# A list schedule for a gated two-layer block: other issue order, folded w_phi, accumulated kv, token-major queries

## The chip, the cores and the metric

The kernel runs on one NeuronCore of a Trainium2 chip, and the metric is the device time of one execution in microseconds (us). The core has a matrix engine (PE, with its weight loads shown as PEld), a vector engine (DVE), an activation engine (ACT), a general engine (POOL) and a queue for transfers (SP). Each takes its own instructions strictly in the order in which the program issues them, and waits for the others by semaphores. Matmul results land in PSUM, which this kernel hands out in eight tiles of up to 512 fp32 columns.

## The reference

There are S = 2048 tokens of D = 512 features. A vector c gives six modulation rows; sa, ca, ga steer the attention half and sb, cb, gb the feed-forward half.

```python
h = _layernorm(x, axis=-1) * (1 + ca) + sa
x = x + ga * _A_ref(h, A_wqkv, A_w_phi, A_wo)
h = _layernorm(x, axis=-1) * (1 + cb) + sb
x = x + gb * _B_ref(h, B_w_gate, B_w_up, B_w_down)
```

`_A_ref` is a linear attention with 32 heads of 16 features. Queries and keys are multiplied by a 16x16 matrix w_phi of their head; phi is the softmax of the result beside the softmax of its negative. For each head kv = sum over tokens of phi_k times v, z = sum of phi_k; the output is (phi_q kv) / (phi_q z + 1e-6), times wo. `_B_ref` is silu(h w_gate) * (h w_up), times w_down, with 1376 hidden features. All keys must be seen before the first query can be finished, and a token's feed-forward half needs its attention output.

## The kernel before

Tokens are handled in 16 tiles of 128 rows, or in 4 chunks of 512. The stages stand in the program in this order, and each engine gets its instructions in that order.

1. **Setup.** The modulation columns come from one-column matmuls (L138). w_phi is folded into wq and wk: 32 transposes (L176), 32 matmuls against a block-diagonal w_phi (L183), with (1 + ca) multiplied into the result (L186) and into wv (L188). The terms with sa become biases: cq for the queries (L192), a row ck added to the keys by a matmul with a row of ones (L200, L266), bv added to kv afterwards (L206, L370). Layernorm statistics of all 16 tiles (L216 to L223) are issued before the first key tile.
2. **Keys.** For each pair of tiles `k_ln_pair` normalises, transposes and copies (L256 to L259); for each tile `k_tile_mm` makes keys and values (L265, L269), two exponentials (L271, L272), the values' copy (L275), head sums (L278), reciprocals (L280) and phik on POOL (L282). phik and vaug are kept for all 16 tiles. Four of the 16 `q_front_j` groups (L291, L295) are placed among the key tiles.
3. **Between.** `prep_mod2`, `prep_bgu`, the multiplication of wg and wu by (1 + cb) on ACT (L347, L348), of wo and wd by their gates on DVE (L351, L356), and `kv_group`: eight runs of 16 matmuls over the token tiles (L365).
4. **Query side of a chunk**, `q_back_gen`: it works feature-major. Sums of the exponentials come from eight matmuls with a selection matrix (L391) and four fp32 transposes (L398); the quotients are made on DVE (L401 to L415), transposed back (L419), spread over the features by eight matmuls with Esel (L428), multiplied into the exponentials (L431) and taken through KVblk (L436); then wo (L446), the residual (L448), the second layernorm (L233) and its transposes (L236, L237).
5. **Feed-forward of a chunk**: 11 groups of `ffn_gu` (L469 gate, L473 up, L476 silu, L479 on DVE or L483 and L484 on ACT and POOL), then 4 `ffn_down` (L492) and the output (L496, or L499 and L500).

The order of 4 among 3 and 5 is written by hand: `plan` mixes the 12 other query groups with the first chunk's `q_back_gen`, and `hooks_m` and `hooks_t` say after which group the next chunk's generator takes a step. The first `ffn_gu` waits for the first chunk's last step.

## Time and profile before

| what | value |
|---|---|
| three timed runs | 277.44, 277.82 and 278.03 us, median 277.82 |
| span of the profiled execution | 275.5 us |
| the profiled execution's own time | not given; the median lies 2.3 us above the span |
| PE busy | 240.7 us, 87% of the span, 1468 matmuls |
| DVE, ACT, POOL busy | 171.8, 138.6, 80.5 us |
| read from memory | 11.58 MB |

The span runs from the first to the last instruction of the profiled execution. Busy is time in which at least one instruction of an engine runs; matmuls overlap, so that the mean time of one (384 ns) is longer than the step from one to the next (four in 0.86 us). An engine's idle time matters only where the end depends on it.

### The profile page before, as it was taken

What the parts mean: (1) busy time and instruction counts of PE and PEld (TensorE: products, weight loads), DVE (VectorE), ACT (ScalarE), POOL (GpSimd) and SP (SyncE); (2) the same over time, 40 slices, a digit from 0 to 9 for tenths busy, and PEclk for the clock granted to TensorE, in tenths of its full rate; (3) what the DMA queues carried; (4) which work ended last, traced back from release to release, by engine and by line L of the source; (5) the groups of instructions that cost most, each with busy time, mean ns of one, the idle gap of its engine ahead of it and who ended that gap; (6) DMA issues with size and microseconds to landing.
All of it is one profiled execution on the core that took longest, in us unless ns stands there. A gap on an engine that the chain in (4) does not pass through costs nothing.

```text
span 275.5 us, 3831 instructions
## 1 busy us (share of the span) xinstructions
PE 240.7 (87%) x1468; PEld 118.5 (43%) x1468; DVE 171.8 (62%) x351; ACT 138.6 (50%) x208; POOL 80.5 (29%) x91
## 2 busy tenths in 40 slices
PE   0499869999799879289999899999899999899993
PEld 0473323433586334234444344444344444444441
DVE  4799899999859946716665627556718555712210
ACT  2297146775696956056691056651055660165500
POOL 2602267576870000102221312230313310233311
PEclk9999999999979979869999999999999999999999
DMA  7999600000000000000000010000000000100001
GB/s 260 385 403 411 228 0 2 0 2 2 0 2 4 0 0 2 0 0 0 0 2 19 19 38 2 0 1 20 33 27 0 0 2 19 38 21 0 0 19 57
DMA packets 10067, 13.91 MB, mean 51 GB/s; under 512 B 993, under 2 KB 6978, under 8 KB 10050
## 3 DMA queue, kind: packets, MB, share of 16 engines
q1 hardware_dynamic: 9522, 13.16, 12.9%
q10 hardware_dynamic: 528, 0.52, 0.6%
q8 instruction: 11, 0.18, 0.3%
q14 instruction: 6, 0.05, 0.1%
HBM read 11.58 MB, written 2.10 MB: 50 GB/s over the span
## 4 chain that ended last, share of the span: by engine, by line
PE 47%; issue 17%; DVE 14%; POOL 8%; ACT 8%; DMA 3%; POOLq 1%; SPq 0%
PE g_ps L469 14%; PE u_ps L473 13%; PE f_ps L492 9%; POOL phik L282 5%; DVE Ssum L278 4%; DMA wqkv_sb<-in_A_wqkv_dram 3%; ACT xn2T L237 3%; POOL ln_rstd L221 3%; DVE Rk L280 2%; PE a_ps L446 2%; PE sdT_ps L391 2%; PE cb_ps L428 2%; PE o_ps L436 2%; DVE ln_st L216 1%; DVE vaug L275 1%
## 5 line engine op out<-in xcount | busy, mean ns | idle before, releaser
L469 PE MATMUL g_ps<-xn2T,wg_sb 128*128 128x512 bf16 (+1 forms) x176 | 46.0, 384 | 2.1 <-ACT xn2T L237 2.0
L473 PE MATMUL u_ps<-xn2T,wu_sb 128*128 128x512 bf16 (+1 forms) x176 | 45.9, 384 | 0.0
L479 DVE SCALAR_TENSOR_TENSOR gu<-u_ps,bgu,sg 128x512 bf16<-128x512 f32 (+1 forms) x24 | 18.0, 750 | 41.7 <-PE u_ps L473 39.5
L484 POOL TENSOR_TENSOR gu<-u_sb,sg 128x512 bf16<-128x512 bf16 x20 | 23.5, 1176 | 69.3 <-ACT u_sb L483 69.3
L476 ACT ACTIVATE sg<-g_ps,bgu 128x512 bf16<-128x512 f32 (+1 forms) x44 | 30.3, 688 | 26.4 <-PE g_ps L469 25.4
L492 PE MATMUL f_ps<-wd_sb,gu 128*128 128x512 bf16 (+1 forms) x176 | 40.2, 379 | 0.0
L282 POOL TENSOR_TENSOR phik<-e_sb,Rk 128x1024 bf16<-128x1024 bf16 x16 | 33.9, 2119 | 14.7 <-DVE Rk L280 13.2
L469 PEld LDWEIGHTS <-wg_sb 128*128 128x128 bf16 (+1 forms) x176 | 17.6, 101 | 22.3 <-issue 4.4
L431 DVE TENSOR_TENSOR phiT<-eT,cb_ps 128x512 bf16<-128x512 bf16 x32 | 20.5, 682 | 10.2 <-PE cb_ps L428 10.2
L473 PEld LDWEIGHTS <-wu_sb 128*128 128x128 bf16 (+1 forms) x176 | 17.9, 101 | 21.0 <-issue 1.1
L492 PEld LDWEIGHTS <-gu 128*128 128x128 bf16 (+1 forms) x176 | 17.1, 98 | 20.1
L221 POOL TENSOR_TENSOR ln_rstd<-ln_veps,mhalf 128x4 f32<-128x4 f32 x8 | 8.1, 1014 | 52.7 <-DVE ln_veps L219 52.7
L500 POOL TENSOR_TENSOR o_sb<-x,f_sb 128x512 bf16<-128x512 bf16 x8 | 9.2, 1152 | 46.1 <-ACT f_sb L499 46.1
L237 ACT COPY xn2T<-xnT_ps 128x1024 bf16<-128x1024 bf16 x8 | 7.7, 1015 | 28.2 <-PE xnT_ps L236 28.2
L278 DVE TENSOR_REDUCE Ssum<-e_sb 128x64 f32<-128x1024 bf16 x16 | 19.3, 1209 | 2.9 <-ACT e_sb L272 2.8
L265 PE MATMUL pk_ps<-Wk,xnT 128*128 128x512 bf16 x64 | 17.2, 379 | 1.7 <-ACT xnT L259 1.1
L499 ACT CAST f_sb<-f_ps 128x512 bf16<-128x512 f32 x8 | 4.7, 593 | 26.7 <-PE f_ps L492 26.7
L269 PE MATMUL v_ps<-Wv,xnT 128*128 128x512 bf16 x64 | 16.9, 381 | 0.7 <-ACT e_sb L272 0.5
L291 PE MATMUL pq_ps<-xnT,Wq 128*128 128x512 bf16 x64 | 17.1, 395 | 0.2 <-ACT e_sb L272 0.2
L271 ACT ACTIVATE e_sb<-pk_ps 128x512 bf16<-128x512 f32 x16 | 9.7, 604 | 14.8 <-POOL phik L282 14.6
L483 ACT ACTIVATE u_sb<-u_ps,bgu 128x512 bf16<-128x512 f32 x20 | 13.8, 688 | 3.0 <-PE u_ps L473 2.6
L446 PE MATMUL a_ps<-wo_sb,oT 128*128 128x512 bf16 x64 | 15.0, 379 | 0.0
(122 smaller groups left out, 364.2 us busy)
## 6 DMA issues: line engine op xcount, KB each, us to landing
wmod_sb<-in_w_mod_dram SPq DMA_DIRECT2D x3, 1024.0 KB, 7.7
out_dram<-o_sb SPq DMA_DIRECT2D x16, 128.0 KB, 1.7
wqkv_sb<-in_A_wqkv_dram SPq DMA_DIRECT2D x1, 1536.0 KB, 9.6
x_c<-in_A_x_dram SPq DMA_DIRECT2D x3, 512.0 KB, 9.7
wg_sb<-in_B_w_gate_dram SPq DMA_DIRECT2D x1, 1376.0 KB, 13.8
wu_sb<-in_B_w_up_dram SPq DMA_DIRECT2D x1, 1376.0 KB, 15.1
wd_sb<-in_B_w_down_dram SPq DMA_DIRECT2D x1, 1280.0 KB, 15.3
x_c<-in_A_x_dram ACTq DMA_DIRECT2D x1, 512.0 KB, 3.4
```

Source lines behind the costliest of these rows:

```text
L265: nc.tensor.matmul(pk_ps[:], lhsT=xnT[:, k, cols], rhs=Wk2[:, k, :], start=(k == 0), stop=False)
L278: nc.vector.tensor_reduce(Ssum[:], e_sb[:], axis=AX.X, op=ALU.add)
L282: nc.gpsimd.tensor_tensor(pk_t[:], e_sb[:], Rk[:].unsqueeze(3).to_broadcast([P, 2, H, DH]), op=ALU.mult)
L291: nc.tensor.matmul(pq_ps[:], lhsT=Wq2[:, k, j * P:(j + 1) * P], rhs=xnT[:, k, cs], start=(k == 0), stop=(k == KD - 1))
L431: nc.vector.tensor_tensor(ph[:], eT[sg][j][:], cb_ps[:], op=ALU.mult)
L446: nc.tensor.matmul(a_ps[:], lhsT=oT[j][:, t * P:(t + 1) * P], rhs=wo_sb[:, j, :], start=(j == 0), stop=(j == KD - 1))
L469: nc.tensor.matmul(g_ps[0:fsz, :], lhsT=wg_sb[:, k, m * P:m * P + fsz], rhs=xn2T[:, k, :], start=(k == 0), stop=(k == KD - 1))
L473: nc.tensor.matmul(u_ps[0:fsz, :], lhsT=wu_sb[:, k, m * P:m * P + fsz], rhs=xn2T[:, k, :], start=(k == 0), stop=(k == KD - 1))
L476: nc.scalar.activation(sgt[0:fsz, :], g_ps[0:fsz, :], ACT.Silu, bias=prep["bgu"][0:fsz, m:m + 1])
L479: nc.vector.scalar_tensor_tensor(gu[0:fsz, :], in0=u_ps[0:fsz, :], scalar=prep["bgu"][0:fsz, FM + m:FM + m + 1], in1=sgt[0:fsz, :], op0=AL ...
L484: nc.gpsimd.tensor_tensor(gu[0:fsz, :], u_sb[0:fsz, :], sgt[0:fsz, :], op=ALU.mult)
L492: nc.tensor.matmul(f_ps[:], lhsT=guT[m][0:fsz, t * P:(t + 1) * P], rhs=wd_sb[0:fsz, m, :], start=(m == 0), stop=(m == FM - 1))
```

## The change

The order of the instructions no longer follows the text of the program. Each stage adds operations to a `Plan`, with an assumed duration, the buffers that it reads and writes, and, for some, a choice of two engines. A list scheduler then simulates the engines at build time with these durations (0.2 us from one engine to another), takes the operation that can start first and among those within 0.15 us the one whose due time is earliest, and emits everything in the order of its simulated starts. Due times are counted back from the end along the matmuls of the keys and the feed-forward half ("spine"), and second-layernorm transposes are spaced by `PACE` = 11 us. PSUM is handed out as six single banks, with quotas by use, and one pair of banks.

What is computed changes too:

- w_phi alone is folded into wq and wk (two plain copies per fold, on ACT). The modulation is applied to the normalised, transposed activations as they leave PSUM, by a scale and a bias per feature. The scalings of wq, wk, wv, wg and wu and all four biases (cq, ck, bv, bgu) are gone.
- kv is summed in three PSUM banks, eight matmuls per key tile as the tile comes, and the ones column of the four reused vaug tiles gives z.
- The query side is token-major: for half a tile of heads (`attend`) four matmuls with the exponentials as stationary operand and a [128, 144] block of KVZ as moving one give numerators, softmax sums and denominators at once, in the pair of banks. Two small copies, four small DVE operations and two DVE multiplications make o2; POOL adds its two halves, PE transposes (`turn`; for the first two tiles PE does both with an identity), ACT copies.
- The first four feed-forward units are pairs of tiles instead of chunks (`UNITS`); two blocks of 256 columns share a bank. All residual additions of the output run on DVE. wo and wd get their gates on POOL, 15 multiplications.
- The loads come in another order and x is laid out with four rows of a chunk per partition; the silu of c is made from an exponential.

The functions printed above are replaced as a whole; the core of what takes their place:

```diff
--- before.py
+++ after.py
...
+UNITS = [(0, 0, 2), (0, 2, 2), (1, 0, 2), (1, 2, 2), (2, 0, 4), (3, 0, 4)]
...
+PACE = 11.0
...
+            cand = {}
+            for o in ready:
+                t0, rooms = o.at, []
+                for b in o.news:
+                    got = self.room(b, live)
+                    if got is None:
+                        t0 = None
+                        break
+                    t0 = max(t0, got[0])
+                    rooms.append((b, got[1]))
+                if t0 is None:
+                    continue
+                for alt in o.alts:
+                    eng = alt[0]
+                    t = max(t0, free[eng])
+                    for p in o.preds:
+                        t = max(t, p.end + (self.HOP if p.eng != eng else self.OWN[eng]))
+                    cand.setdefault(eng, []).append((t, o.due, o.n, o, alt, rooms))
+            best = None
+            for eng, cs in cand.items():
+                first = min(c[0] for c in cs) + SLACK
+                c = min((c for c in cs if c[0] <= first), key=lambda c: c[1:3])
+                if best is None or c[:3] < best[:3]:
+                    best = c
...
+    ctx.enter_context(tc.manual_schedule())
...
+    slots = {"one": 6, "two": 1, "xn": 8, "nmr": 4, "ln2": 6, "WT": 2, "e": 3, "S": 3, "R": 3, "phik": 4,
+             "va": 4, "Ssw": 2, "A": 2, "o2": 3, "o": 2, "oT": 2, "sg": 3, "gu": 13,
+             "usb": 2, "ot": 3}
+    quota = {"q": 1, "turn": 1, "T": 2, "wo": 1, "down": 2, "gu": 4, "kv": 4, "fold": 3}
...
+    at_x[0] = load(nc.sync, x_ch[0][:], x_v[0], 512)
+    at_wk = load(nc.sync, wqkv_sb[:, :, D:2 * D], wqkv_v[:, :, D:2 * D], 512)
+    at_m1 = load(nc.sync, wmod_sb[:, :, 0:2 * D], wmod_v[:, :, 0:2 * D], 1024)
+    at_wv = load(nc.sync, wqkv_sb[:, :, 2 * D:3 * D], wqkv_v[:, :, 2 * D:3 * D], 512)
+    at_x[1] = load(nc.sync, x_ch[1][:], x_v[1], 512)
+    at_wq = load(nc.sync, wqkv_sb[:, :, 0:D], wqkv_v[:, :, 0:D], 512)
+    at_x[2] = load(nc.sync, x_ch[2][:], x_v[2], 512)
+    at_x[3] = load(nc.sync, x_ch[3][:], x_v[3], 512)
+    at_m2 = load(nc.sync, wmod_sb[:, :, 2 * D:6 * D], wmod_v[:, :, 2 * D:6 * D], 2048)
+    at_wo = load(nc.sync, wo_sb[:], A_wo.rearrange("(k p) n -> p k n", p=P), 512)
+    at_wg = load(nc.sync, wg_sb[:], B_w_gate.rearrange("(k p) n -> p k n", p=P), 1376)
+    at_wu = load(nc.sync, wu_sb[:], B_w_up.rearrange("(k p) n -> p k n", p=P), 1376)
+    load(nc.sync, wd_sb[:, 0:FM - 1, :], B_w_down[0:(FM - 1) * P, :].rearrange("(m p) n -> p m n", p=P), 1280)
...
+    def fold_phi(col0, W2, bW2, bw):
+        WTb = sb("prep", "WT", [P, KD, D], BF16)
+        parts = [Buf() for _ in range(KD)]
...
+            pl.op("PE", r=[bw], w=[tp], us=0.24, fn=ft)
+            pl.op("ACT", r=[tp], w=[WTb, parts[j]] if j == 0 else [parts[j]], us=0.49,
+                  fn=lambda j=j, tp=tp: nc.scalar.copy(WTb()[:, j, :], tp()[:].rearrange("p i m -> p (i m)")))
+        for i in range(KD):
+            pp = bank("fold")
+            def fb(i=i, pp=pp):
+                for j in range(KD):
+                    nc.tensor.matmul(pp()[:, j * P:(j + 1) * P], lhsT=WTb()[:, j, i * P:(i + 1) * P],
+                                     rhs=BD[:, j].rearrange("p h f -> p (h f)"), start=True, stop=True)
+            pl.op("PE", r=parts + [WTb, bBD], w=[pp], us=0.24, fn=fb)
+            pl.op("ACT", r=[pp], w=[bW2[i]], us=0.49, fn=lambda i=i, pp=pp: nc.scalar.copy(W2[:, i, :], pp()[:]))
...
+        pl.op([("ACT", 0.48 + 0.21 * w, lambda: evac(True)), ("DVE", 0.4 + 0.13 * w, lambda: evac(False))],
+              r=[tp, bmod], w=[bdst[2 * jp], bdst[2 * jp + 1]])
...
+        pk, v = bank("kv"), bank("kv")
...
+        pl.op("PE", r=h_bufs(i) + bWk2, w=[pk], us=0.865, fn=fk, spine=True)
...
+        pl.op("ACT", r=[pk], w=[e], us=0.98, fn=fe)
+        pl.op("PE", r=h_bufs(i) + [bwv], w=[v], us=0.865, fn=fv, spine=True)
...
+        pl.op([("ACT", 0.49, lambda: fva(nc.scalar.copy)), ("DVE", 0.66, lambda: fva(nc.vector.tensor_copy))],
+              r=[v], w=[bva[i]])
+        Ss, R = sb("kph", "S", [P, 2, H], FP32), sb("kph", "R", [P, 2, H], FP32)
+        pl.op("DVE", r=[e], w=[Ss], us=1.18, fn=lambda: nc.vector.tensor_reduce(Ss()[:], e()[:], axis=AX.X, op=ALU.add))
+        pl.op("DVE", r=[Ss], w=[R], us=0.5, fn=lambda: nc.vector.reciprocal(R()[:], Ss()[:]))
+        bphik[i] = sb("kph", "phik", [P, 2, H, DH], BF16)
+        pl.op("POOL", r=[e, R], w=[bphik[i]], us=1.9, fn=lambda: nc.gpsimd.tensor_tensor(
+            bphik[i]()[:], e()[:], R()[:].unsqueeze(3).to_broadcast([P, 2, H, DH]), op=ALU.mult))
...
+    def kv_tile(i):
+        def f():
+            for g in range(G):
+                sg, j = divmod(g, KD)
+                nc.tensor.matmul(kv_acc(g // 3)[:, (g % 3) * (P + 1):(g % 3 + 1) * (P + 1)],
+                                 lhsT=bphik[i]()[:, sg, 8 * j:8 * j + 8, :].rearrange("p h f -> p (h f)"),
+                                 rhs=bva[i]()[:, j, :], start=(i == 0 and g % 3 == 0), stop=(i == NT - 1),
+                                 skip_group_check=True)
...
+        pl.op("PE", r=hb + bWq2, w=[pq], us=0.865, fn=f)
+        for sg in range(2):
+            beT[c_i, sg, j] = Buf()
+            pl.op("ACT", r=[pq], w=[beT[c_i, sg, j]], us=0.49, fn=lambda sg=sg: nc.scalar.activation(
+                eTs[c_i, sg, j][:], pq()[:], ACT.Exp, scale=(1.0 if sg == 0 else -1.0)))
...
+                pl.op("POOL", r=[bgab[0]], w=[bwo[k]], us=1.13, fn=lambda k=k: nc.gpsimd.tensor_tensor(
+                    wo_sb[:, k, :], wo_sb[:, k, :], gab[:, 0, :], op=ALU.mult))
...
+                pl.op("POOL", r=[bgab[1]], w=[bwd[m]], us=1.13, fn=lambda m=m, fsz=fsz: nc.gpsimd.tensor_tensor(
+                    wd_sb[0:fsz, m, :], wd_sb[0:fsz, m, :], gab[0:fsz, 1, :], op=ALU.mult))
...
+        nd = pair()
+        js = [half * HK + jj for jj in range(HK)]
+        def fn():
+            for jj, j in enumerate(js):
+                for sg in range(2):
+                    nc.tensor.matmul(nd()[:, jj, sg * NDW:(sg + 1) * NDW], lhsT=eTs[c_i, sg, j][:, ts_],
+                                     rhs=KVZ[:, sg * KD + j, :], start=True, stop=True)
+        pl.op("PE", r=[beT[c_i, sg, j] for j in js for sg in range(2)] + bKVZ + [bturn], w=[nd], us=0.25, fn=fn)
...
+            U = pools["qf"].tile([P, HK, 2, 8], FP32, name="U", bufs=2)
+            nc.vector.tensor_tensor(U[:], ndv()[:, :, :, P + 8:P + 16], Ssw()[:], op=ALU.mult)
+            den = pools["qf"].tile([P, HK, 8], FP32, name="den", bufs=2)
+            nc.vector.tensor_tensor(den[:], U[:, :, 0, :], U[:, :, 1, :], op=ALU.add)
+            rden = pools["qf"].tile([P, HK, 8], FP32, name="rden", bufs=2)
+            nc.vector.reciprocal(rden[:], den[:])
+            nc.vector.tensor_tensor(A()[:], Ssw()[:], rden[:].unsqueeze(2).to_broadcast([P, HK, 2, 8]), op=ALU.mult)
...
+        def fo():
+            for sg in range(2):
+                nc.vector.tensor_tensor(o2()[:, sg, half * HK:(half + 1) * HK, :].rearrange("p j (h d) -> p j h d", d=DH),
+                                        ndv()[:, :, sg, 0:P].rearrange("p j (h d) -> p j h d", d=DH),
+                                        A()[:, :, sg, :].unsqueeze(3).to_broadcast([P, HK, 8, DH]), op=ALU.mult)
...
+            pl.op("POOL", r=[o2, second], w=[o], us=1.15, fn=lambda: nc.gpsimd.tensor_tensor(
+                o()[:], o2()[:, 0], o2()[:, 1], op=ALU.add))
+            pl.op("PE", r=[o], w=[tp], us=0.23, fn=f)
+        pl.op("ACT", r=[tp], w=[oT], us=0.49, fn=lambda: nc.scalar.copy(oT()[:], tp()[:]))
...
+        pl.op("PE", r=[oT] + bwo, w=[a], us=0.865, fn=f)
+        xs = x_ch[c_i][:, t, :]
+        pl.op("DVE", r=[a, bx[n]], w=[bx[n]], us=0.66, fn=lambda: nc.vector.tensor_tensor(xs, xs, a()[:], op=ALU.add))
...
+        bxn2[n] = normalize(xs, mv, rstd_t, bn, nmr_t, 0, [bx[n], mv])
...
+        pl.op("PE", r=hb + [bwgu], w=[g], us=us, fn=lambda: f(g, wg_sb), spine=True)
+        pl.op("PE", r=hb + [bwgu], w=[u], us=us, fn=lambda: f(u, wu_sb), spine=True)
+        pl.op("ACT", r=[g, bsilu], w=[sg], us=0.2 + 0.3 * L / CW, fn=lambda: nc.scalar.activation(
+            sg()[0:fsz, 0:L], g()[0:fsz, 0:L], ACT.Silu))
+        if (ms[0] * w // TPC) % 2 == 0:
+            pl.op("DVE", r=[u, sg], w=[gu], us=0.1 + 0.55 * L / CW, fn=lambda: nc.vector.tensor_tensor(
+                gu()[0:fsz, 0:L], u()[0:fsz, 0:L], sg()[0:fsz, 0:L], op=ALU.mult))
         else:
+            usb = sb("qf", "usb", [P, CW], BF16)
+            pl.op("ACT", r=[u], w=[usb], us=0.2 + 0.3 * L / CW, fn=lambda: nc.scalar.copy(
+                usb()[0:fsz, 0:L], u()[0:fsz, 0:L]))
+            pl.op("POOL", r=[usb, sg], w=[gu], us=0.1 + 1.05 * L / CW, fn=lambda: nc.gpsimd.tensor_tensor(
+                gu()[0:fsz, 0:L], usb()[0:fsz, 0:L], sg()[0:fsz, 0:L], op=ALU.mult))
...
+        pl.op("DVE", r=[fp, bx[n]], w=[ot], us=0.66, fn=lambda: nc.vector.tensor_tensor(
+            ot()[:], x_ch[c_i][:, t, :], fp()[:], op=ALU.add))
+        pl.op("SP", r=[ot], us=0.05, fn=lambda: nc.sync.dma_start(out_v[c_i, :, t, :], ot()[:]))
...
+    def prepare(k):
+        a, b = 2 * k, 2 * k + 1
+        attend(a, 0)
+        attend(a, 1)
+        attend(b, 0)
+        turn(a, k == 0)
+        attend(b, 1)
+        project(a)
+        turn(b, k == 0)
+        project(b)
+        h2_guard(k)
...
+    for unit in UNITS:
+        c_i, t0, w = unit
+        last = (c_i * TPC + t0 + w) // 2
+        guT = {}
+        nm = TPC // w
+        while done < last:
+            prepare(done)
+            done += 1
+        for ms in [list(range(m, min(m + nm, FM - 1))) for m in range(0, FM - 1, nm)] + [[FM - 1]]:
+            ffn_gu(unit, ms, guT)
+        for t in range(t0, t0 + w):
+            ffn_down(unit, t, guT)
+    for fn in pl.run():
+        fn()
```

## The prediction

> **What bounds the kernel now.** I read the page's head, then the busy time by stage, then the chain of waits and the timeline at the stage borders.

> ```profile
> span 275.5 us, 3831 instructions
> PE 240.7 (87%) x1468; PEld 118.5 (43%) x1468; DVE 171.8 (62%) x351; ACT 138.6 (50%) x208; POOL 80.5 (29%) x91
> ```

> PE is the bound on average. The stages (start:end, length, then busy time and count of PE, PEld, DVE, ACT, POOL, granted clock, transfers):

> ```profile
> 0.00:22.00 22.00, 11.16 (x140) 8.62 (x141) 15.56 (x49) 11.20 (x20) 6.18 (x24) 1.00 0.95 352
> 22.00:34.50 12.50, 11.17 (x53) 4.18 (x52) 11.18 (x34) 4.93 (x7) 3.61 (x19) 1.00 0.81 309
> 34.50:81.00 46.50, 41.12 (x364) 21.07 (x363) 41.74 (x65) 31.04 (x48) 33.91 (x16) 0.96 0.01 1
> 81.00:110.40 29.40, 26.71 (x183) 13.90 (x180) 22.28 (x60) 21.21 (x32) 0.00 (x0) 0.94 0.01 1
> 110.40:118.60 8.20, 1.99 (x17) 1.73 (x17) 4.90 (x15) 1.93 (x3) 1.01 (x1) 0.78 0.00 0
> 118.60:161.10 42.50, 41.24 (x196) 18.90 (x196) 23.50 (x41) 21.23 (x31) 7.93 (x7) 0.96 0.03 10
> 201.70:242.30 40.60, 39.33 (x196) 18.53 (x196) 23.38 (x41) 17.19 (x27) 9.32 (x8) 1.00 0.04 13
> 242.30:271.00 28.70, 28.67 (x132) 13.01 (x131) 5.88 (x8) 12.04 (x18) 8.08 (x7) 1.00 0.06 19
> 271.00:275.50 4.50, 0.00 (x0) 0.00 (x0) 0.00 (x0) 0.59 (x1) 1.15 (x1) 0.99 0.08 29
> ```

> The start (22 us) waits for loads and folds weights. In the key stage, 34.5 to 81, DVE is busy 41.7 of 46.5 us. 110.4 to 118.6 is a gap: everything waits for the first chunk's second layernorm. From 118.6 on PE sets the pace. Unit prices of PE come from the chain of waits (first row) and the timeline:

> ```profile
> 123.81 0.86 PE g_ps L469 x4
> ```
> ```profile
> 81.80 4.16 PE L365 MATMUL kv_ps<-vaug,phik 128*128 128x129 bf16 x70
> 118.63 1.87 PE L469 MATMUL g_ps<-xn2T,wg_sb 128*128 128x512 bf16 x4 [1.16 <-ACT xn2T L237]
> ```

> A 512-column matmul steps every 0.86 / 4 = 0.215 us; a 129-column one every 4.16 / 70, nearly 0.058 (its own end included). After the gap four cost 1.87 us: a gap is paid twice.

> **What the change takes off PE and adds to it.**

> ```profile
> L428 PE MATMUL cb_ps<-chlT,Esel 128*128 128x512 bf16 x32 | 10.4, 393 | 0.7 <-ACT chlT L421 0.7
> L436 PE MATMUL o_ps<-phiT,KVblk 128*128 128x512 bf16 x32 | 10.1, 384 | 0.0
> L391 PE MATMUL sdT_ps<-eT,selz 128*128 128x512 bf16 x32 | 8.2, 379 | 0.1
> L266 PE MATMUL pk_ps<-ck_row,ones_row 1*128 1x512 bf16 x16 | 6.1, 384 | 0.0
> L398 PE MATMUL sd_ps<-ident_f,sdT 128*128 128x128 f32 x16 | 2.5, 276 | 0.0
> L334 PE MATMUL bgu_ps<-sb_bf,wg_sb 128*128 128x1 bf16 (+1 forms) x44 | 1.3, 165 | 1.5 <-DVE sb_bf L317 1.5
> ```

> Gone: 32 + 32 + 32 + 16 matmuls of 512 columns and 8 more for ck and bv, 120 x 0.215 = 25.8 us; the fp32 transposes 2.5; 16 transposes of the quotients, 0.9; 136 one-column matmuls (two bgu groups at 1.3, cq, half of modB), about 4. New: 128 matmuls of 144 columns at 0.058 x 144 / 129 = 0.065, 8.3 us; the turns, 56 transposes and 16 identity matmuls at 0.058, 4.2 us. Net 33.2 - 12.5 = about 21 us less PE work. The pairs of 256 columns double the count of gate and up matmuls in half of the tokens, but not their columns; bounds nothing (by columns) to 176 x 0.03 = 5 us (one-column row, 1.3 / 44 each, on top); I take nothing, because weight loads already run beside matmuls at 129 columns.

> The kv row shows 0.058 us per small matmul with a weight load each. [...]

> **A, the start.** The first key matmul moves from 22.17 us forward:

> ```profile
> 7.18 1.01 PE L138 MATMUL modA_ps<-silucT,wmod_sb 128*128 128x1 bf16 x32 [3.75 <-DMA wmod_sb<-in_w_mod_dram]
> 11.22 1.03 PE L176 MATMUL wT_ps<-ident_b,wqkv_sb 128*128 128x128 bf16 x8 [3.03 <-DMA wqkv_sb<-in_A_wqkv_dram]
> ...
> 22.17 1.03 PE L265 MATMUL pk_ps<-Wk,xnT 128*128 128x512 bf16 x4
> ```

> By 7.18 us 1.5 MB had landed (x_c0 and a third of w_mod), by 11.22 another 1.5 MB: 0.37 MB per us. Now x_c0 and wk (1 MB) come first, by about 5.8; 1 MB of w_mod by about 8.6. Wk's fold is four transpose groups, four ACT copies, four matmul groups, four ACT copies, each copy 0.594 us (row L185 below): 5.8 + 0.6 + 2.4 + 0.3 + 2.4 = 11.5. modA: 8.6 + 1.0 + copies 0.3 + the scaled copy out of PSUM 1.0 = 10.9, hidden under the fold. SP issues its transfers in this order without a wait, c and w_phi go by ACT's queue. No weights are scaled and no statistics of later chunks stand ahead in DVE's queue (before: 22 to 32 us). I take **12** (11 to 17: a transfer late by half the present order).

> **B, keys and queries.** PE: 48 groups of four (16 keys, 16 values, 16 queries) x 0.86 = 41.3; kv 128 x 0.058 = 7.4; 64 transposes 3.7; the fold of Wq 1.9; modB and gates 2.7: 57 us. The other engines by tile:

> ```profile
> L278 DVE TENSOR_REDUCE Ssum<-e_sb 128x64 f32<-128x1024 bf16 x16 | 19.3, 1209 | 2.9 <-ACT e_sb L272 2.8
> L280 DVE RECIPROCAL Rk<-Ssum 128x64 f32<-128x64 f32 x16 | 8.6, 540 | 0.1
> L216 DVE BATCH_NORM_STATS2 ln_st<-x 128x6 f32<-128x512 bf16 x16 | 10.9, 688 | 0.2
> L275 DVE CAST vaug<-v_ps 128x512 bf16<-128x512 f32 x16 | 10.8, 677 | 0.0
> L256 DVE TENSOR_SCALAR xn<-x_c,ln_rstd,ln_nmr 128x512 bf16<-128x512 bf16 x16 | 7.7, 495 | 0.0
> ```
> ```profile
> L272 ACT ACTIVATE e_sb<-pk_ps 128x512 bf16<-128x512 f32 x16 | 9.6, 600 | 0.0
> L185 ACT CAST WBD_u<-wbd_ps 128x512 bf16<-128x512 f32 x8 | 4.2, 594 | 0.5 <-PE wbd_ps L183 0.3
> L282 POOL TENSOR_TENSOR phik<-e_sb,Rk 128x1024 bf16<-128x1024 bf16 x16 | 33.9, 2119 | 14.7 <-DVE Rk L280 13.2 <-ACT e_sb L272 1.1 <-DVE sb_bf L317 0.3
> ```

> DVE: 1.21 + 0.54 + 0.69 + 0.2 small + 0.5 = 3.1 us a tile, 50 us; ACT: four exponentials 2.4 and the modulated copy 0.6 = 3.0, 48 us, and 10 copies for Wq and gates, 6 us; the value copy (0.68) goes to either. POOL: 2.1 x 16 plus 15 gate multiplications at half a phik, 1.06 each, 50 us; wd's are wanted only by the first down. Each of four engines has 50 to 57 us, so no wait is covered by much: what waits late next is phik on POOL, and behind it kv_tile on PE's queue and all behind that. I add 4: **61** (57 to 72: 72 if the old pace, 46.5 / 16 = 2.9 us a tile, has the query group, 0.86, and a value copy, 0.68, put on top: 4.5 x 16).

> **C, from the last kv to the first gate matmul.** KVZ about 2 us. Then four `attend` halves in a row, for there is one pair of banks: each four matmuls 0.26, two tiny copies, four small DVE operations, about 0.9 for the six, two 256-element multiplications at 0.41, two handovers 0.5: 2.5 us, 10 in all. These come from

> ```profile
> L403 DVE TENSOR_TENSOR Tq<-Rq,sd_ps 128x256 f32<-128x256 f32 x4 | 1.6, 408 | 0.0
> L219 DVE TENSOR_SCALAR ln_veps<-ln_mv 128x4 f32<-128x4 f32 x8 | 1.3, 163 | 0.1
> L221 POOL TENSOR_TENSOR ln_rstd<-ln_veps,mhalf 128x4 f32<-128x4 f32 x8 | 8.1, 1014 | 52.7 <-DVE ln_veps L219 52.7
> ```

> (bounds for a half: 1.9 without handovers, 4.9 if each handover queues behind one feed-forward instruction). Then turn 0.5, copy 0.6, wo 0.9, residual 0.7, statistics 0.9, rstd with its two small ones 1.3, xn 0.5, transposes 0.3, copy 0.9, handovers 1.6: 8. Sum 20. Query groups held back fill some 5 of it, and the slow clock behind the gap costs 2: **17** (10 to 24). First gate matmul at 12 + 61 + 17 = 90, before 118.6.

> **D, the rest.** 528 matmuls x 0.215 = 113.5; the other 14 tiles' attends 7.3, turns 3.2, wo 56 x 0.215 = 12.0, transposes 3.2: 139 us. The chunk of 40.6 us above holds 172 x 0.215 + 36 x 0.058 = 39.1 us of such work, 4% lost; with as much, **145** (139 to 158). The loss was the layernorm at the chunk's end, now spread; what replaces it is queueing on DVE, whose attends (32 x 1.7 = 54 us) and output sums come in place of the feature-major quotients.

> **E, the tail.** 4.5 us, less 0.59 on ACT and 1.15 on POOL, plus 0.68 on DVE: **3.5**.

> Sum 12 + 61 + 17 + 145 + 3.5 = 238.5. The median of the runs is 2.3 us above the span (277.8 against 275.5), so 240.8; I say **240**.

> **The rivals.** *The holes close*: the static order packs B at 57, C at 10, D at 140: 12 + 57 + 10 + 140 + 3.5 + 2.3 = 225. For: the order is made for it; against: durations assumed at build time differ (copies 0.49 against 0.594 in row L185), and every engine is strictly in order. *The attend loop becomes the bound*: with one pair of banks, the 28 halves after the first pair's four come one after another, from 81 us on (90 less the layernorm part, 9, during which they may begin). With L us a half, the last chunk's feed-forward part (28.7 us, the window from 242.3) and a layernorm, 8, follow: 81 + 28 L + 37 + 5.8. It decides above L = 4.1; at the upper bound 4.9 it gives 261. *Slower than before*, by that same loop, from L = 5.5 on: 28 x 5.5 + 124 = 278. For: three handovers a half, each behind a queue of 0.7 to 0.9 us instructions; against: halves alone are 2.5. *The change doesn't do what it says*: the issue order is kept, but late instructions hold their queues, B 70, C 20, D 155: 263.

> **How the numbers follow.** The sum as it stands 0.58 (its own range 231 to 251); holes closed 0.18; the loop as bound 0.08; late order 0.10; slower 0.05; the remaining 0.01 is no change, where 0.2% is what a measurement of this kernel can tell. Faster 0.94, same 0.01, slower 0.05. The range takes the closed holes and the loop at its bound: 225 to 261.

> **What would show it.** The first key matmul near 12 us; the last kv near 73; the first gate matmul near 90, with a low granted clock just before; PE matmul columns 21 us cheaper; attends 2.5 to 3 us apart; the last matmul near 235. The prediction is wrong if PE idles over 10 us inside D (then the waits name DVE or the pair of banks), or if B runs over 70 us with PE waiting for phik.

## The result and the profile after

The changed kernel takes **247.8 us** (median of 4 runs, 246.5 to 248.5), the kernel before 277.9 in the same session: a ratio of 0.892 (95% interval 0.888 to 0.896). The forecast was 240 with a range of 225 to 261. The profiled execution took 248.46 us with a span of 246.7. A few executions of a kernel come out more than 1.5% slower than its best one; times and ratios here and below are of the others.

The head of the page after, and the busy times of its stages, cut where the prediction's terms end: A to the first key matmul, B to the last kv product, C to the first gate matmul, D to the last matmul, E to the end (columns as before: start:end, length, busy time and count of PE, PEld, DVE, ACT, POOL, granted clock, transfers).

```profile
span 246.7 us, 4221 instructions
PE 215.0 (87%) x1533; PEld 131.7 (53%) x1556; DVE 174.6 (71%) x461; ACT 128.3 (52%) x280; POOL 101.1 (41%) x100
```
```profile
0.00:14.40 14.40, 7.01 (x79) 5.80 (x81) 8.94 (x35) 6.36 (x11) 2.61 (x14) 1.00 0.91 320
14.40:72.10 57.70, 49.88 (x393) 29.56 (x397) 50.54 (x78) 42.86 (x79) 45.55 (x30) 0.94 0.33 122
72.10:92.20 20.10, 14.65 (x92) 7.61 (x92) 16.27 (x61) 10.62 (x24) 6.01 (x7) 0.92 0.00 1
92.20:243.30 151.10, 143.51 (x974) 88.72 (x987) 98.17 (x289) 68.46 (x167) 46.89 (x50) 1.00 0.04 14
243.30:246.70 3.40, 0.00 (x0) 0.00 (x0) 0.69 (x1) 0.00 (x0) 0.00 (x0) 1.00 0.11 39
```

PE is busy 25.7 us less than before (240.7); some 2 us of this are 23 matmuls that this profile lacks (another of the same kernel has all 1556 and 217.4 us). The gap that stood at 110 to 118 us is gone. By term, measured against forecast: A 14.4 against 12, B 57.7 against 61, C 20.1 against 17, D 151.1 against 145, E 3.4 against 3.5, around the span 1.76 against 2.3. The differences, +2.4 −3.3 +3.1 +6.1 −0.1 −0.5, add up to the 7.7 us by which this execution passed the 240.8 of the sum.

**B is not PE's.** The chain of waits (start, length, what), from the key stage:

```profile
19.66 1.29 DVE ln_veps L353
20.95 1.13 DVE S L548
...
22.66 1.08 DVE S L548
23.74 1.01 DVE ln_nmr L361
...
36.52 2.25 DVE xn L372 x2
```

From 17 to 58 us the chain hardly leaves DVE: PE waits for DVE here, though both are busy for some 50 of 57.7 us. And some of what DVE is "busy" with is standing still. `ln_nmr` handles 4 elements per partition and takes 1.01 us. The timeline around 49 us shows what holds it (first DVE, then POOL):

```profile
47.77 1.16 DVE L548 TENSOR_REDUCE S<-e 128x64 f32<-128x1024 bf16 x1
48.85 1.10 DVE L361 SCALAR_TENSOR_TENSOR ln_nmr<-ln_mv,ln_rstd 128x4 f32<-128x4 f32 x1
49.87 0.54 DVE L549 RECIPROCAL R<-S 128x64 f32<-128x64 f32 x1
50.34 3.56 DVE L372 TENSOR_SCALAR xn<-x_c,ln_mv,ln_rstd 128x512 bf16<-128x512 bf16 x2
```
```profile
48.00 5.74 POOL L551 TENSOR_TENSOR phik<-e,R 128x1024 bf16<-128x1024 bf16 x3
```

POOL's three phik end near 49.9, 51.8 and 53.74. `ln_nmr` ends at 49.95, and the two `xn`, 0.41 us each elsewhere, end at 53.90. The reduction S and the reciprocal R beside the same phik take 1.16 and 0.54 us (1.15 to 1.22 and 0.52 to 0.55 over the whole span). So in this stretch `ln_nmr` and `xn` stood still until POOL's running instruction ended, and S and R did not.

### The profile page after: what moved, and what is told of

Same layout as the page of the kernel before. It is cut to its first block, busy times and chain, and to the rows that moved or that the text cites. A ratio compares the mean times of both kernels' runs of the same rounds, so it can differ in the third digit from the quotient of the medians.

```text
span 246.7 us, 4221 instructions
## 1 busy us (share of the span) xinstructions
PE 215.0 (87%) x1533; PEld 131.7 (53%) x1556; DVE 174.6 (71%) x461; ACT 128.3 (52%) x280; POOL 101.1 (41%) x100
## 4 chain that ended last, share of the span: by engine, by line
PE 64%; DVE 24%; ACT 3%; DMA 3%; issue 3%; POOL 1%; SPq 0%; DVEq 0%; ACTq 0%
PE one_ps L786 31%; PE one_ps L818 14%; DVE S L548 5%; PE one_ps L748 5%; PE two_ps L675 3%; DVE st L343 3%; DMA wmod_sb<-in_w_mod_dram 3%; DVE xn L372 3%; PE one_ps L528 2%; PE one_ps L575 2%; DVE R L549 2%; PE one_ps L532 2%; DVE o L707 2%; ACT hT L396 2%; DVE ln_nmr L361 1%
## 5 line engine op out<-in xcount | busy, mean ns | idle before, releaser
L786 PE MATMUL one_ps<-hT,wg_sb 128*128 128x256 bf16 (+3 forms) x264 | 46.2, 308 | 1.2 <-ACT hT L396 0.9
L786 PE MATMUL one_ps<-hT,wu_sb 128*128 128x256 bf16 (+3 forms) x260 | 45.2, 307 | 0.2
L793 ACT ACTIVATE sg<-one_ps 128x512 bf16<-128x512 f32 (+2 forms) x46 | 26.3, 577 | 28.3 <-PE one_ps L786 25.2
L802 POOL TENSOR_TENSOR gu<-usb,sg 128x512 bf16<-128x512 bf16 (+1 forms) x22 | 23.5, 1070 | 42.7 <-ACT usb L800 39.9
L818 PE MATMUL one_ps<-wd_sb,gu 128*128 128x512 bf16 (+1 forms) x171 | 40.5, 379 | 0.2
L551 POOL TENSOR_TENSOR phik<-e,R 128x1024 bf16<-128x1024 bf16 x16 | 30.7, 1931 | 13.0 <-ACT hT L396 5.5
L707 DVE TENSOR_TENSOR o<-two_ps,A 128x256 bf16<-128x256 f32 x64 | 24.0, 416 | 0.8
L343 DVE BATCH_NORM_STATS2 st<-x_c 128x6 f32<-128x512 bf16 x32 | 21.7, 679 | 2.7 <-DMA x_c<-in_A_x_dram 2.4
L581 ACT ACTIVATE eT<-one_ps 128x512 bf16<-128x512 f32 x32 | 17.5, 599 | 10.3 <-PE one_ps L575 10.3
L675 PE MATMUL two_ps<-KVZ,eT 128*128 128x144 bf16 x128 | 13.7, 232 | 7.3 <-DVE o L707 6.9
L548 DVE TENSOR_REDUCE S<-e 128x64 f32<-128x1024 bf16 x16 | 19.1, 1191 | 1.3 <-ACT e L539 1.2
```

Source lines behind the costliest of these rows:

```text
L343: nc.vector.bn_stats(st6[:], src)
L548: pl.op("DVE", r=[e], w=[Ss], us=1.18, fn=lambda: nc.vector.tensor_reduce(Ss()[:], e()[:], axis=AX.X, op=ALU.add))
L551: pl.op("POOL", r=[e, R], w=[bphik[i]], us=1.9, fn=lambda: nc.gpsimd.tensor_tensor(bphik[i]()[:], e()[:], R()[:].unsqueeze(3).to_broadcast ...
L675: nc.tensor.matmul(nd()[:, jj, sg * NDW:(sg + 1) * NDW], lhsT=eTs[c_i, sg, j][:, ts_], rhs=KVZ[:, sg * KD + j, :], start=True, stop=True)
L707: nc.vector.tensor_tensor(o2()[:, sg, half * HK:(half + 1) * HK, :].rearrange("p j (h d) -> p j h d", d=DH), ndv()[:, :, sg, 0:P].rearrang ...
L786: nc.tensor.matmul(ps_()[0:fsz, q * n:(q + 1) * n], lhsT=wt[:, k, m * P:m * P + fsz], rhs=h2[k], start=(k == 0), stop=(k == KD - 1))
```

## The experiments

**The changed kernel again**, on one chip with `e2_no_gates`, `e3_norm_on_act` and `e4_wphi_first`.

> The changed kernel itself, for comparison on the same chip as the next three. 247 to 249 us. It tells no theories apart; what the others gain or lose is measured against it.

248.1 us, ratio 0.891 (0.883 to 0.899); span 246.7 again, and the stage borders of the first profile to within 0.6 us. D is 151.1 us again, which makes its length a fine gauge for runs with the same order.

### What the order is worth

`e1_text_order` issues the instructions in the order of the text.

```diff
-                first = min(c[0] for c in cs) + SLACK
-                c = min((c for c in cs if c[0] <= first), key=lambda c: c[1:3])
+            nxt = min(o.n for o in ready)
+            best = min((c for cs in cand.values() for c in cs if c[2] == nxt), key=lambda c: c[0])
...
-        return [fn for _, _, fn in sorted(order, key=lambda x: x[:2])]
+        return [fn for _, _, fn in order]
```

> The changed kernel with every engine's instructions issued in the order in which the program's text makes them; the same arithmetic, the same tiles. Theory O, the order carries the gain of the stage after the kv sum: all 16 query groups run in the key stage, so the chain from the last kv product to the first gate matmul stands alone (20 us with PE idle for most of it), and each of the 7 later pairs is prepared ahead of a feed-forward unit with nothing under it, some 13 us more each: 247 + 7 x 13 = 338, from 315 to 365. Theory W, the smaller work carries it and the order is worth little, since the engines run apart as far as their semaphores let them: 250 to 275.

413.7 us, ratio 1.490 (1.478 to 1.502): the same arithmetic without the schedule is half as slow again as the kernel before. Its last stages by windows, and what PE waited for over the whole span (total, times, longest):

```profile
115.60:133.20 17.60, 7.96 (x48) 4.97 (x48) 12.08 (x47) 1.77 (x4) 1.10 (x2) 0.63 0.00 0
133.20:412.90 279.70, 181.73 (x984) 100.35 (x983) 113.39 (x308) 62.57 (x155) 46.91 (x50) 0.73 0.02 8
```
```profile
PE two_ps L671 <- DVE o L703: 41.1, 24, 2.1
PE one_ps L731 <- POOL o L732: 32.0, 14, 4.2
PE one_ps L384 <- DVE xn L368: 29.5, 10, 5.5
```

Theory O holds in kind. Its size was short, by 49 us against its upper bound: not only does each pair's preparation stand alone, the granted clock is lower too (0.63 and 0.73 in these two stages, 0.77 in the mean), and PE's busy time grows from 217 to 266 us. In this text order the new arithmetic loses 136 us against the kernel before, and the list schedule brings 166. A text order arranged by hand, like that of the kernel before, was not tried.

### What POOL and DVE cost each other

`e2_no_gates` leaves out the 15 multiplications of wo and w_down by their gates (so the output is that of ungated weights), every other instruction in its place.

```diff
-                pl.op("POOL", r=[bgab[0]], w=[bwo[k]], us=1.13, fn=lambda k=k: nc.gpsimd.tensor_tensor(
-                    wo_sb[:, k, :], wo_sb[:, k, :], gab[:, 0, :], op=ALU.mult))
+                pl.op("POOL", r=[bgab[0]], w=[bwo[k]], us=1.13, fn=lambda: None)
...
+                pl.op("POOL", r=[bgab[1]], w=[bwd[m]], us=1.13, fn=lambda: None)
```

> Leaves out the 15 multiplications of wo and wd by their gates on POOL; the place of every other instruction in its queue is the same. Theory P (POOL and DVE exclude each other on some operations, so that a multiplication on POOL holds up DVE: normalisations of 2.0 us instead of 0.41, the small operations 0.8 instead of 0.2): the key stage loses 3 to 6 us of DVE's stalls and the first attend, 3.5 us, comes down to 2.7, so 242 to 245 us. Theory D (the key stage is paced by DVE's own work, 43 us without the long rows, and by the order): POOL had 12 us idle there, so 247 to 249 as before.

243.4 us, ratio 0.876 (0.869 to 0.883). B, C and D of its profile:

```profile
13.20:67.20 54.00, 47.74 (x398) 27.55 (x397) 49.51 (x80) 42.82 (x79) 33.63 (x19) 1.00 0.38 141
67.20:85.80 18.60, 13.64 (x94) 6.92 (x92) 15.29 (x61) 10.62 (x24) 1.10 (x2) 1.00 0.01 1
85.80:236.90 151.10, 144.31 (x989) 88.62 (x987) 98.26 (x289) 68.41 (x167) 46.82 (x50) 1.00 0.04 14
```

Leaving out work on an engine that was never the longest gave 4.8 us against the changed kernel beside it; in the profiled executions B is 3.7 us shorter, C 1.5, and A, which the edit doesn't touch, 1.2. DVE loses only 1 us of busy time in B and in C. The other difference is the granted clock: 1.00 throughout, where the changed kernel has 0.94 and 0.92. This run doesn't separate the two. Two later ones, `e8_second_norm_act` and `e9_less_dve`, have the changed kernel's key stage, multiplications and all, and lost less to the clock in it (0.97 in B). Their B is 56.5 us, 1.2 shorter than the changed kernel's, so part of the 3.7 us is the clock.

`e3_norm_on_act` gives the nine first-layer normalisations of DVE to ACT, in the same places of the order.

```diff
-        pl.op([("DVE", 0.6, fd), ("ACT", 0.71, fa)], r=list(reads) + [bn], w=[bxn])
+        pl.op([("DVE", 0.6, fa if act_only else fd), ("ACT", 0.71, fa)], r=list(reads) + [bn], w=[bxn])
```

> The nine first-layernorm normalisations that the schedule gives to DVE run on ACT instead, at the same place in the order. Theory P: DVE's stalls behind phik on POOL go (896 instead of 407 ns in the mean, 4.4 us in sum), and the 3.9 us in which PE stands at 50 to 54 us with them; ACT gets 7 us more work of 16 us that it idles in the stage: 243 to 246 us. Theory D: the work only changes engines, DVE loses 3.7 us and ACT is late with exponentials: 247 to 250.

248.3 us, ratio 0.894 (0.888 to 0.901): no gain, as theory D had it. Its B and C:

```profile
13.70:69.40 55.70, 49.37 (x398) 27.75 (x397) 42.39 (x70) 47.90 (x87) 45.39 (x30) 1.00 0.36 133
69.40:91.30 21.90, 16.26 (x93) 8.32 (x92) 16.27 (x61) 10.73 (x25) 6.00 (x7) 0.84 0.00 1
```

DVE is freed of 8.2 us in B, B is 2 us shorter, and C takes 1.8 of them back, at a granted clock of 0.84. With DVE at 42.4 of 55.7 us, its busy time alone no longer sets B; PE's longest waits there are now for `xn` from ACT (2.5 us in all).

`e5_down_gates_later` and `e6_later_and_act` let the w_down multiplications start only after the first pair's second transposes; the second also gives all first-layer normalisations to ACT. The schedule makes a new order for both.

```diff
+    for m in range(FM):
+        fsz = fm_size(m)
+        pl.op("POOL", r=[bgab[1]] + bh2[0], w=[bwd[m]], us=1.13, fn=lambda m=m, fsz=fsz: nc.gpsimd.tensor_tensor(
+            wd_sb[0:fsz, m, :], wd_sb[0:fsz, m, :], gab[0:fsz, 1, :], op=ALU.mult))
```

> The 11 multiplications of the down weights by their gate may begin only when the second normalisation's first pair is ready, so they leave the key stage and the chain behind it (about 12.8 us of POOL) for the first feed-forward unit, where DVE has 11 of 39 us free. The list schedule makes a new order with that. Theory P, a running POOL instruction holds back DVE's SBUF-only instructions, and this costs the key stage and the chain about 5 us: the part of the 4.75 us that leaving out all 15 gained, 11/15 of it or 3.5 us, is kept: 243.5 to 246, with the first gate matmul at 87 to 90. Theory R, the stalls go with the multiplications wherever they run, or the first down product waits for them: 247 to 250.

> As the run before, and the first layer norm's 16 normalisations are all given to ACT in the plan (DVE is no choice). Theory P: the key stage loses the DVE stalls of 7 us that xn showed, the last kv product comes at 67 to 69 and, with no gate multiplications in the chain, the first gate matmul at 86 to 88: 241 to 244. Theory R: 246 to 249, as when nine normalisations alone went to ACT (248.3).

248.0 us (0.895, 0.888 to 0.902) and 247.0 us (0.889, 0.884 to 0.894), three executions each: neither differs from the changed kernel. Yet B is 54.0 and 51.7 us long, 3.7 and 6.0 shorter. Their D:

```profile
87.10:241.20 154.10, 146.19 (x989) 89.06 (x987) 100.02 (x288) 68.25 (x167) 57.67 (x60) 0.99 0.04 14
```
```profile
86.40:241.80 155.40, 147.06 (x989) 89.53 (x987) 99.02 (x286) 68.06 (x166) 57.77 (x60) 0.98 0.04 14
```

Theory P was right on the key stage and wrong on the time: 3.0 and 4.3 us come back in D, some 2 and 3 of it as PE work that takes longer (146.2 and 147.1 us against 144.3), at a granted clock of 0.99 and 0.98. Both runs have another order in D too, so they don't show the cause alone.

### Smaller questions

`e4_wphi_first` loads w_phi at the head of the same queue as x (`nc.scalar.dma_start` to `nc.sync.dma_start`).

> w_phi is the first transfer on SP's queue instead of the second on ACT's; all other queues unchanged. If the start is 2.4 us later than predicted because DVE stands in BD waiting for w_phi (landed at 8.1 us) with the first normalisation and then ACT's fourth copy of the fold behind it: first key matmul 1 to 2 us earlier, 246 to 247 us. If the 1 MB of w_mod (landed at 9.3) is what the first key waits for, or if the 512 small pieces of w_phi delay x: no gain, 247 to 249.

249.9 us, ratio 0.899 (0.892 to 0.905). BD is made 0.8 us sooner and the first key matmul comes no sooner (14.6): w_mod now lands at 10.07 instead of 9.28, and PE's order has the fold's second half behind it.

`e7_measured_times` puts the durations of the profile into the plan (for instance):

```diff
-        pl.op("ACT", r=[pk], w=[e], us=0.98, fn=fe)
+        pl.op("ACT", r=[pk], w=[e], us=1.15, fn=fe)
```

> The changed kernel with the plan's durations set to those of its own profile (two exponentials 1.15 in place of 0.98, ACT copies of 512 columns 0.60 for 0.49, normalisation on DVE 0.41 for 0.60 and on ACT 0.81 for 0.71, the evacuations of the transposes 1.13 for 0.90 us on ACT and so on); the list schedule makes a new order with them. Theory M, the 6 us by which the last stage and the chain exceeded my terms come from an order planned on short durations: 242 to 245. Theory P, they come from what no duration of one instruction holds (DVE and POOL excluding each other, one pair of PSUM banks for all attends): 246.5 to 249.5.

253.5 us, ratio 0.911 (0.903 to 0.918): slower than the order made with the old durations, and outside what either theory expected. B is 60.1 and D 154.0 us. Better prices don't make a better order here. Neither the exclusion of POOL and DVE nor the clock is in the plan; that this is the reason, no run shows.

`e8_second_norm_act` moves 12 of DVE's second-layer normalisations to ACT in the same places; `e9_less_dve` moves 6 gate-by-up products to POOL besides.

```diff
-        pl.op([("DVE", 0.6, fd), ("ACT", 0.71, fa)], r=list(reads) + [bn], w=[bxn])
+        pl.op([("DVE", 0.6, fa if on_act else fd), ("ACT", 0.71, fa)], r=list(reads) + [bn], w=[bxn])
...
+                u2 = pools["qf"].tile([P, CW], BF16, name="u2", bufs=2)
+                nc.scalar.copy(u2[0:fsz, 0:L], u()[0:fsz, 0:L])
+                nc.gpsimd.tensor_tensor(gu()[0:fsz, 0:L], u2[0:fsz, 0:L], sg()[0:fsz, 0:L], op=ALU.mult)
```

> Every engine's order as in the changed kernel, but the 12 normalisations of the second layer norm for the tokens from 256 on that DVE made (0.41 us each) run on ACT at the same places (0.81 us each). Theory V, between 131 and 177 us DVE has no time left (38.9 us busy of 45.8, and the rest are gaps between instructions) and this is what leaves PE idle for 5 us there: DVE loses 3 us in that stretch, PE waits 2 to 3 us less, first gate matmul to last product 148 to 149.5 in place of 151.1, the time 245 to 246.5. Theory L, the one pair of banks that all attends share sets the pace by its chain of some 2.7 us, whatever DVE does beside it: 151, the time 247.5 to 249, or later since a normalisation takes 0.4 us longer on its own path.

> As the run before, and in the two feed-forward units of the second 512 tokens (from about 134 to 176 us) the 6 gate-by-up multiplications that DVE made go to POOL, behind a copy on ACT. Theory V: another 4.1 us off DVE in the stretch: first gate matmul to last product 146.5 to 148.5, the time 243.5 to 246. Theory P with V: the 7 us more of POOL hold back DVE's instructions on SBUF, so no more than the run before, 148 to 150. Theory L: 151 to 153, the time 247.5 to 250.

251.4 us (0.906, 0.899 to 0.913) and 256.9 us (0.926, 0.920 to 0.931). Theory V is refuted. What PE waited for from 92 us on, in the changed kernel and then in `e8_second_norm_act`:

```profile
PE two_ps L675 <- DVE o L707: 2.8, 2, 1.7
PE one_ps L388 <- DVE xn L372: 1.8, 2, 1.3
PE one_ps L748 <- ACT oT L739: 0.9, 2, 0.7
PE one_ps L786 <- ACT hT L396: 0.9, 2, 0.4
```
```profile
PE two_ps L675 <- DVE o L707: 3.3, 2, 1.7
PE one_ps L388 <- ACT xn L376: 2.9, 2, 1.9
```

With 4.4 us less on DVE, D is 155.0 us: these waits grow by 1.6, and PE's busy time is 2.0 us longer (146.3 against the 144.3 of `e2_no_gates`) at a granted clock of 0.99. In `e9_less_dve` the same two grow to 5.5 and 3.5 us and D to 160.9, more than any of its theories expected. What PE misses in D is the length of each pair's path (one attend after the other through one pair of banks, then the normalisation), not time on DVE: a step made slower on a free engine lengthens the path.

### Where the gains went

`e10_gates_in_gaps` keeps the order of the changed kernel on every engine but POOL; there the 11 w_down multiplications go where POOL stands idle, from the last phik on (a helper `wd_gates(count)` issues the next of them).

```diff
+            if i == NT - 1:
+                wd_gates(2)
...
+                if rstd_n[0] == 2:
+                    wd_gates(2)
...
+                wd_gates(3 if n == 2 else 2)
...
+                wd_gates(1)
```

> PE, DVE, ACT and SP keep the changed kernel's order; on POOL the 11 multiplications of the down weights move out of the key stage to places where POOL stands idle: 2 behind the last phik, 2 behind the first pair's normalisations, 3 and 2 behind the next two sums of o, the last 2 behind the first products gu. Theory P: the key stage ends 3 to 4.5 us earlier (last kv product 67.5 to 69), the chain takes 19 to 20 us, and the rest keeps its 151.1 us, since it keeps its order: 243 to 245, where leaving out all 15 gave 243.4. Theory R, DVE's stalls return where the multiplications go, or the first down products wait for them: the rest takes 153 to 155 and the time is 246.5 to 249.

248.5 us, ratio 0.890 (0.881 to 0.899). B is 55.6 us, C 21.6, D 153.0: again a shorter key stage and nothing in the end. In C theory R's stalls returned: beside the moved multiplications the first pair's `xn` at 86.52 us takes 1.34 us (0.41 in the changed kernel), and DVE is busy 2 us longer. PE's timeline shows where 2 us of D went. First the changed kernel ahead of its last unit, then this one:

```profile
213.38 0.56 PE L388 MATMUL one_ps<-ident_b,xn 128*128 128x128 bf16 x7 [1.34 <-DVE xn L372]
214.37 1.26 PE L786 MATMUL one_ps<-hT,wg_sb 128*128 128x512 bf16 x4 [0.43 <-ACT hT L396]
```
```profile
211.72 0.57 PE L394 MATMUL one_ps<-ident_b,xn 128*128 128x128 bf16 x7 [1.34 <-DVE xn L378]
212.72 1.40 PE L805 MATMUL one_ps<-hT,wg_sb 128*128 128x512 bf16 x4 [0.43 <-ACT hT L402]
213.91 1.92 PE L805 MATMUL one_ps<-hT,wu_sb 128*128 128x512 bf16 x4
```

The same two gaps, 1.34 and 0.43 us. Behind them the changed kernel's matmuls run at full clock, and in this one four of them take 1.92 us. Windows give the granted clock (the sixth figure after the length), the changed kernel's and this one's. The last two of each are 3.41 us long and cut at whole multiples of 3.41 us from the beginnings of that execution's spells of half clock, which the last section lists:

```profile
54.00:56.00 2.00, 1.45 (x15) 1.45 (x14) 2.00 (x5) 0.00 (x0) 0.91 (x1) 0.50 0.00 0
...
78.00:80.00 2.00, 1.63 (x8) 0.79 (x7) 1.34 (x5) 0.83 (x2) 0.00 (x0) 0.50 0.00 0
...
209.86:213.28 3.42, 2.18 (x14) 1.01 (x12) 2.77 (x7) 1.02 (x2) 0.55 (x1) 1.00 0.11 38
213.28:216.69 3.41, 2.75 (x16) 1.42 (x18) 0.85 (x4) 1.62 (x3) 0.00 (x0) 1.00 0.11 38
```
```profile
88.00:90.00 2.00, 2.00 (x11) 1.17 (x12) 1.73 (x7) 1.02 (x2) 0.00 (x0) 0.50 0.00 0
...
210.30:213.71 3.41, 1.57 (x13) 0.83 (x12) 2.01 (x7) 1.02 (x2) 0.55 (x1) 1.00 0.11 38
213.71:217.13 3.42, 3.42 (x10) 1.22 (x8) 0.69 (x1) 0.60 (x1) 0.00 (x0) 0.50 0.00 0
```

The changed kernel has half clock at 53 to 60 us, in the stretch that DVE bounds, and at 77 to 80; this run has it for 3.4 us each from 53, 87 and 214 us, and behind the last two the chain of work runs on PE.

`e12_gaps_and_fills` is that kernel with matmuls that nobody reads in two of the gaps.

```diff
+            if fill and jp == 0:
+                for _ in range(7 if mod is modB and dst is hT[0] else 5):
+                    nc.tensor.matmul(one_ps[tp.slot][:], lhsT=ident_b[:], rhs=wo_sb[:, 0, :], start=True, stop=True)
```

> The run with the down weights' multiplications in POOL's gaps, and beside it matmuls whose result nobody reads, in two places where that run's trace has PE idle ahead of a spell of half clock: 7 of 512 columns (1.5 us) ahead of the first pair's transposes, where PE stood 1.88 us for xn, and 5 (1.1 us) ahead of the last pair's, where it stood 1.34 us. Theory H, what moving those multiplications gained in the key stage was given back through PE's clock, which fell to half behind these two gaps and stretched the products that followed by 1.3 and 2 us: the chain from the last kv product to the first gate matmul 20.0 to 20.5 in place of 21.6, from there to the last product 151 in place of 153.0, granted clock 0.99, the time 243 to 245.5. Theory R, the gain goes elsewhere, and the added matmuls only stand in the way: 246.5 to 249.

**245.8 us**, ratio 0.885 (0.881 to 0.890). Its C and D:

```profile
68.80:89.20 20.40, 15.08 (x100) 7.56 (x99) 17.39 (x62) 10.96 (x24) 4.87 (x6) 1.00 0.00 1
89.20:240.20 151.00, 145.36 (x994) 89.11 (x992) 99.21 (x288) 68.28 (x167) 54.52 (x57) 1.00 0.04 14
```

Theory H holds for both places: C lost 1.2 us and D 2.0, with 12 matmuls more on PE and nothing else changed. (A came 1.4 us later in this execution, because w_mod landed 0.7 us later and PE kept its slow pace of the start longer (the first value product took 1.71 us, 1.08 in `e10_gates_in_gaps`), and B took 1.3 less, without its spell at 53 us; the edit explains neither, and the two cancel.) One execution could owe this to chance. But the six of this run have mean clocks of 0.986 to 0.999, and the three of `e10_gates_in_gaps` that count 0.979 to 0.993. The median is 0.3 us above the theory's range. It is the fastest version with the full computation; it was timed against the kernel before and not beside the changed kernel, and the two intervals (to 0.890, from 0.883) overlap, so that a gain of about 2 us is likely rather than proven.

## Why the prediction was right or wrong, step by step

**PE's work, right.** Forecast 21 us less, measured 23.3 less (217.4 of 240.7, from the profile that has all matmuls). Up to 1.7 of these are not work: the kernel before spent 13.7 us at half clock and this one 10.2, and half of the difference is 1.7. The pairs of 256 columns cost nothing, as taken: the chain of waits has

```profile
102.84 5.24 PE one_ps L786 x48
```

0.109 us each, half of 0.215 to within 2 ns. Six kv products stepped through 0.35 us in the chain (at 61.56 us), 0.058 us each, as before.

**A, 2.4 us short.** A was to have modA "hidden under the fold", and it was not. PE has one queue, and the order puts the fold's second half behind modA's columns, which wait for w_mod:

```profile
1.65 7.63 DMA wmod_sb<-in_w_mod_dram
9.32 1.02 PE one_ps L434 x32
10.34 0.88 PE one_ps L388 x8
11.21 1.71 PE one_ps L475 x16
12.92 0.43 PE one_ps L532
```

The loads landed 0.7 us after the 8.6 forecast, what I had put side by side stands in a row, and a value product runs ahead of the first key. That `e4_wphi_first` moved w_phi forward for nothing agrees. The larger part of the miss is something else that the sum lacked: at the start PE runs at about half of its later pace. The eight transposes at 10.34 us take 0.88 us, and eight at 111.58 us take 0.45. The four matmuls of the first value product took 1.71 us in the second profile of the changed kernel, and 0.87 in that of `e10_gates_in_gaps`, whose first key matmul came at 13.1 us; later on four take 0.86. (The granted clock reads 1.00 over this stage and doesn't show it.) At the later pace the row above would end at about 12.6 us, an estimate from 9.32 + 1.02 + 0.45 + 0.90 + 0.86.

**B, 3.3 us shorter, on a wrong ground.** The term was PE's 57 us plus 4. PE had 49.9, since only four of the 16 query groups ran before the last kv product. What set the stage was the chain through DVE. That DVE was busy for the 50 us which the prediction had worked out is luck: some 8.5 of them are standing still (nine `xn` at 896 ns for 407, three `ln_nmr` at 1134 and three `ln_veps` at 567 for the 163 that both took before), so its work was less than forecast. That the term came out only 3.3 us off is luck too, and it hid part of what the other terms missed. That DVE stands still beside POOL, those 8.5 us, was missing altogether, and so was the spell of half clock (6.8 us of B, granted clock 0.94 in its mean). It was the missing mechanism, not the rival "late order"; PE did wait, 3.9 us at 50.6, but for DVE and not for phik.

**C, 3.1 us longer.** The failed step is "query groups held back fill some 5 of it". They did more: nine of the 16, 7.7 us, ran in C. But C is a chain through DVE, and PE work beside a chain shortens some other stage and not the chain; the 5 should not have come off. The other terms held: KVZ 1.2 us against 2, the four halves from 73.3 to 85.0, 11.7 against 10, the rest 7.2 against 8. The slow clock and POOL's hold lie inside these, with 1.5 us together by C without the multiplications, where I had put 2 for the clock. The attends' starts (the first step is 0.8 us longer, the time that `den` and `A` stood behind POOL's multiplications of w_down):

```profile
73.29 0.41 PE L675 MATMUL two_ps<-KVZ,eT 128*128 128x144 bf16 x4 [0.31 <-DVE KVZ L645]
76.78 0.64 PE L675 MATMUL two_ps<-KVZ,eT 128*128 128x144 bf16 x4 [2.22 <-DVE o L707]
79.50 0.64 PE L675 MATMUL two_ps<-KVZ,eT 128*128 128x144 bf16 x4 [0.37 <-DVE o L707]
```

**D, 6.1 us longer.** PE work 139 was forecast and 144.3 measured (`e2_no_gates`, which kept all records): 2.6 us of it are the last three query groups; for the other 2.7 I have only a guess, the modelled ends of small groups, which busy time counts. On top PE stood for 6.8 us, 6.4 of them in the four waits listed above, where I had 6 lost from the chunk before. So the lost share was right and the work was short: I had counted all query groups in B, taken 5 us of them off C, and put none into D.

**The rivals.** The loop of attends did not become the bound: halves 2.7 to 3.5 us apart, where 4.1 decides. It is the largest of D's waits all the same. "The holes close" did not come either: B and C have shorter forms (51.7 and 18.6 us), though not in one kernel.

## What to carry to other kernels

A stage's bound is the engine on which the chain of waits runs, not the one with the longest work, and work that fills a chain's idle time comes off the stage it left and not off the chain. A gain upstream can vanish in PE's clock, as in `e10_gates_in_gaps`, where the same two gaps (1.34 and 0.43 us) as in the changed kernel stood ahead of 3.4 us at 0.50 instead of 1.00: compare the granted clock in windows of 2 us, and PE's idle time ahead of a spell, before looking for a new wait. A list schedule is worth what its model holds; here it lacked POOL's hold on DVE and the clock, and better durations alone made it worse (253.5 us). Whether a plan with both would do better was not tried.
